# Row 28 of K and the last row copies in an adaLN block: from SBUF ahead of attention to DRAM and the first attention steps

## The chip, the cores and the metric

The kernel runs on one core of a Trainium2 chip. The metric is the device time of one launch in microseconds (us), as the median of several runs. The core has five engines that run their own instruction streams: PE (TensorE, matmuls), DVE (VectorE), ACT (ScalarE), POOL (GpSimd) and SP (SyncE). SP only issues DMA transfers here; sixteen DMA engines carry them. A stream runs in order, and an instruction waits for semaphores that other streams and transfers raise.

## What is computed

One transformer block with adaptive layer norm over 2048 tokens of width 448, in float32 (cut to what matters):

```
mod = (silu(c) @ w_mod).reshape(1, 6, 1, 448)       # sa, ca, ga, sb, cb, gb
h = layernorm(x) * (1 + ca) + sa
q, k, v = split(h @ wqkv)                           # 16 heads of width 28
p = softmax(q @ k.T * 28 ** -0.5)
x = x + ga * ((p @ v) @ wo)
h = layernorm(x) * (1 + cb) + sb
x = x + gb * (gelu(layernorm(h) @ w1 + b1) @ w2 + b2)
```

## The kernel before

Matmuls are done to nearly float32 accuracy with operands split in a high and a low part: three products instead of one.

**Phase 1** (to about 170 us) goes through the tokens in four blocks of 512 and computes Q, K and V. Heads are taken in four groups of four. In a group's tile of 128 rows, head j has rows 32j to 32j + 27. Q's four groups and K's groups 0 to 2 are projected directly; the four spare rows of each 32 in these seven carry pieces of K's fourth group, which is put together from them by copies inside DRAM. V stays in SBUF. High and low parts of Q and K go to DRAM arrays `dscr[kind][part][g]` (kind 0 is Q, 1 is K; part 0 is high, 1 low), which the order below calls d000 to d113, in that order of digits.

Three helpers of this phase issue on SP's queue:

- `put_spare` copies the spare rows of the groups and parts that were stored since the last call into the two arrays of K's group 3 (d103 and d113), one transfer of 4 x 4 x 512 for each part. `qk_task` calls it after it has stored a block, so each task's rows are copied one task later.
- `put_ones(g)` writes ones into row 28 of each head of group g in K's high part. They stand there because of the maxima: softmax subtracts a row's maximum, and that maximum, negated, is put in row 28 of Q (`max_fin`, L512), so that the score matmul itself subtracts it. The ones come from a strip of four partitions of the SBUF tile d0, read eight times over.
- `put_last_rows` does the same for group 3, in block 1 of phase 1.

The tile d0 is also scratch for some of phase 1's maxima, and in attention it is the first of three tiles (d0, c0, c1) that take the exponentials.

**Attention** has 16 units (four groups by four blocks of 512 queries) of 16 steps, each step 128 keys. In a step PE computes scores for two heads at a time (L1163, three products; the first has 29 rows, with the ones and the maxima), ACT takes the exponential into the tile (L1168, two to a step), and PE multiplies the step before's exponentials with V (L1133). There are two score tiles, s1 and s0, in turn, in the banks that phase 1's projections used. In between PE and DVE compute the maxima of groups to come, three or four in a step (`emit_max`: matmul L466, reduction L471). Step 0 also holds the last V projection task, on PE behind both score tiles.

Work is put at a step with a table: `at(step, fn)`, and `sched` is read at the end of each step's code. SP has no steps: its stream is the transfers in the order in which the code issues them. K is loaded by `load_k` (L653), Q of a unit by `load_q`, the high parts for the maxima by `load_hi` (L494), the output weights `wo` by a `Prep` object (four transfers for each of four groups, into three buffers `raw`).

**Lanes.** SP's transfers count on eight semaphores, DMAHW0 to DMAHW7, in turn: a transfer's lane is the one after its predecessor's. A transfer waits for the earlier one on its own lane, where that isn't known to be done, and for lanes of transfers whose data it reads or overwrites.

Between phase 1 and attention the code of before issues `load_hi` for what is deferred, then:

```
    put_spare()
    put_ones(1)
    put_ones(2)
```

The ones of group 0 are put in phase 1, in the third task of the last block.

Of the kernel before, what the change touches and what calls it, by code (L numbers as in the profile page):

```python
# [13 lines left out]
F32 = mybir.dt.float32  # L14
# [7 lines left out]
S = 2048  # L22
D = 448
H = 16
DH = 28
# [14 lines left out]
def tile_adaln_block(ctx: ExitStack, tc: tile.TileContext, x, wqkv, wo, w1, b1, w2, b2, c, w_mod, out):  # L40
    nc = tc.nc
    pe, act, dve, pool, sp = nc.tensor, nc.scalar, nc.vector, nc.gpsimd, nc.sync
# [22 lines left out]
    dr = ctx.enter_context(tc.tile_pool(name="dr", bufs=1, space=DRAM))  # L65
# [4 lines left out]
    def nm(t):  # L70
        uid[0] += 1
        return f"{t}_{uid[0]}"

    def sbt(tag, shape, dt=F32, bufs=1):
        return sb.tile(shape, dt, tag=tag, name=nm(tag), bufs=bufs)
# [32 lines left out]
    def f(t):  # L108
        return t.bitcast(F32)
# [226 lines left out]
    def v_init(i):  # L336
# [4 lines left out]
    dscr = [  # L341
        [[dr.tile([128, S], F32R, tag=f"d{kind}{part}{g}", name=f"d{kind}{part}{g}", bufs=1) for g in range(NG)] for part in range(2)]
        for kind in range(2)
    ]
# [5 lines left out]
    def by_head(t):  # L350
        return t.rearrange("(j r) n -> j r n", r=32)

    ones = d0[0:4, 0, 128:384]
    pool.memset(ones, 1.0)

    def put_ones(g):
        sp.dma_start(
            f(dscr[1][0][g])[DH:128:32, :].rearrange("j (q r) -> j q r", r=256),
            ones[:, None, :].broadcast_to([4, 8, 256]),
        )  # L360


    spare = []
# [1 line left out]
    def put_spare():  # L365
        for kind, g, sl in spare:
            n = 4 * (4 * kind + g)
            for part in range(2):
                sp.dma_start(
                    by_head(f(dscr[1][part][3]))[:, n : n + 4, sl], by_head(f(dscr[kind][part][g]))[:, DH:32, sl],  # L370
                )
        spare.clear()


    def put_last_rows():
        for part in range(2):
            sp.dma_start(
                by_head(f(dscr[1][part][3]))[:, DH:32, :].rearrange("j r (q n) -> j (r q) n", n=256),
                ones[:, None, :].broadcast_to([4, 32, 256]),
            )  # L380

    def mm_acc(p, terms, mid=None):
        for i, (a, b) in enumerate(terms):
            if mid and i == len(terms) // 2:
                mid()
            pe.matmul(p, a, b, start=(i == 0), stop=(i == len(terms) - 1))  # L386
# [11 lines left out]
    def qk_terms(b, kind, g, ps=None):  # L398
        ts = terms448(
            *hT[b],  # L400
            lambda k: wq[kind][0](k)[:, 128 * g : 128 * g + 128], lambda k: wq[kind][1](k)[:, 128 * g : 128 * g + 128],
        )
        return (ps or ps_s)(), [(w, h) for h, w in ts]

    def qk_task(b, kind, g, begun=None):
        p, ts = begun or qk_terms(b, kind, g)
        if begun is None:
            mm_acc(p, ts, p1_n[3])
        emit_task(*p1_n[:3])
        if g == 0:  # L410
            tg = ("kh" if kind else "qh") + str(b)
            hi = sb.tile([128, 512], F32R, tag=tg, name=nm(tg), bufs=1)
            (kh_sb if kind else qh_sb)[(g, b)] = hi
        elif g == 1 and b < 2:

            hi = sbt("raw" if kind else "osb", [128, 512], F32R, bufs=3 if kind else 2)
            (kh_sb if kind else qh_sb)[(g, b)] = hi
        else:
            hi = sbt("hi", [128, 512], F32R, bufs=3)
        full = sbt("full", [128, 512], bufs=3)  # L420
        lo = sbt("lo", [128, 512], F32R, bufs=3)
        act.copy(full, p)

        def split():
            (act.copy if b else dve.tensor_copy)(hi, full)
            if kind == 1 and (g, b) == (0, 1):
                k_diff.append(sbt("raw", [128, 512], F32R, bufs=3))
                pool.tensor_tensor(out=k_diff[0], in0=f(hi), in1=f(kh_sb[(0, 0)]), op=ALU.subtract)
            pool.tensor_tensor(out=lo, in0=full, in1=f(hi), op=ALU.subtract)
            sl = slice(b * 512, (b + 1) * 512)  # L430
            for part, t in enumerate((hi, lo)):
                sp.dma_start(f(dscr[kind][part][g])[:, sl], f(t))

            if (b, kind, g) != (3, 0, 3):
                put_spare()
            spare.append((kind, g, sl))

        return split
# [51 lines left out]
    def load_hi(kind, g, b):  # L490
        tg = ("kh" if kind else "qh") + str(b)
        t = sb.tile([128, 512], F32R, tag=tg, name=nm(tg), bufs=1)
        (kh_sb if kind else qh_sb)[(g, b)] = t
        sp.dma_start(f(t), f(dscr[kind][0][g])[:, b * 512 : (b + 1) * 512])  # L494
# [81 lines left out]
    def emit_task(n, sixth, n_pairs):  # L576
        if not n:
            return
        pairs = [pxq.pop(0) for _ in range(min(n_pairs, len(pxq)))]
        rests = [pair_diff(*m) for m in pairs]  # L580
        js = [m[3] for m in pairs]
        n_ops = n - len(pairs) + (sixth and len(pairs) > 0)
        singles = []
        for x in range(n_ops - len(pairs)):
            if mxq:

                free = [j for j in range(4) if j not in js] or range(4)
                fits = [y for y, m in enumerate(mxq[:16]) if m[:3] == mxq[0][:3] and m[4] == free[x % len(free)]]
                singles.append(mxq.pop(fits[0] if fits else 0))
        ops = [lambda ps, m=m: max_one(*m, ps) for m in singles]  # L590
        ops[2:2] = rests
        for x, op in enumerate(ops):
            op(ps_o if x + len(pairs) == 5 else ps_mx)
        for g, qt, cch, i, j in singles:
            count(g, qt, [cch])
        for g, qt, i, j in pairs:
            count(g, qt, [0, 1])
# [98 lines left out]
    for b in range(NB):  # L696
# [12 lines left out]
        for n, (tb, kind, g) in enumerate(tasks):  # L709
# [45 lines left out]
            if b == 1 and n == 8:  # L755
                put_last_rows()
# [10 lines left out]
            if not more:  # L767
                if n == 0:
                    load_q(0)
                    load_q(1)  # L770
                if n == 4:
                    load_k(0, 0)
                    load_k(0, 1)
                if n == 5:
                    act.activation(cols[:, 0:1], zero_col, AF.Exp)
                if n == 2:
                    put_ones(0)
# [29 lines left out]
    phase1[0] = False  # L807
    for item in deferred:
        load_hi(*item)
    put_spare()  # L810
    put_ones(1)
    put_ones(2)
    for g in range(1, NG):
        for qt in range(NB):
            for cch in range(NB):
# [245 lines left out]
    def at(step, fn):  # L1061
        sched.setdefault(step, []).append(fn)
# [10 lines left out]
    def b2_mul():  # L1073
        b2_row = sbt("row_b2g", [128, D])
        pool.tensor_tensor(out=b2_row, in0=rows["b2"][:, :D], in1=rows["gb"], op=ALU.mult)
        rows["b2g"] = b2_row

    at(12, b2_load)
    at(28, b2_mul)
    last0 = NKT * (NU - 1)  # L1080
# [41 lines left out]
    def n_maxima(s_):  # L1122
        n_plain, n_wo = left_steps(s_)
        over = len(mxq) - 7 * n_plain // 2
        if is_wo(s_):
            return max(0, -(-over // max(n_wo, 1)))
        plain[0] += 1
        return 4 if plain[0] % 2 or (over > 3 * n_wo and over > 0) else 3
# [11 lines left out]
    for u in range(NU):  # L1140
        g, qt = divmod(u, NB)
        for kt in range(NKT):
# [10 lines left out]
            n = n_maxima(step)  # L1153
# [81 lines left out]
    for n in range(len(seq) + LAG):  # L1235
        if n < len(seq):
            b, i = seq[n]
# [53 lines left out]
```

## Time and profile before

| | us |
|---|---|
| median of 3 runs | 1146.52 |
| lowest and highest run | 1146.39, 1147.67 |
| the profiled execution, its own time | 1146.45 |
| its span in the trace | 1144.7 |
| PE busy in the span | 1127.3 |
| DVE busy | 833.4 |
| ACT busy | 671.1 |

The profiled execution's time is 1.75 us above its span. Busy times are sums over the whole span, and PE's matmuls are pipelined, so that a busy PE is not PE at its peak. The page also gives the span in 40 equal slices of 28.6 us: the busy share of each engine in tenths, and the clock granted to PE. A wait is idle time of an engine right before an instruction, put down to what was last to end by the trace among the things that it waits for. SPq is SP's queue of DMA issues; a row of it is the issue, not the transfer.

### The profile page before, as it was taken

The page shows a single profiled execution, that of the slowest core. Times are in us where ns is not written, and L with a number is a line of the kernel's source. Part 1 is how long each engine was busy: PE and PEld are TensorE (multiplying, and loading weights), DVE is VectorE, ACT ScalarE, POOL GpSimd, SP SyncE. Part 2 cuts the span into 40 slices and gives each one's busy share as a digit, 9 for nine tenths or more (in the row PEclk, how much of TensorE's full clock was granted, in tenths as well). Part 3 has the DMA queues.
Part 4 walks back from the last instruction along what each step waited for, and adds up shares of the span by engine and source line. Part 5 has one row for each costly group of instructions (what it writes and reads, how often), then busy time and mean ns, then how long its engine had stood idle before and what let it go on. Part 6 is the DMA issues. An engine that isn't in the chain of part 4 may idle for free.

```text
span 1144.7 us, 20656 instructions
## 1 busy us (share of the span) xinstructions
PE 1127.3 (98%) x8319; PEld 674.3 (59%) x8319; DVE 833.4 (73%) x1485; ACT 671.1 (59%) x823; POOL 209.6 (18%) x211
## 2 busy tenths in 40 slices
PE   9999998999999999999999999999999999999998
PEld 6756663444444444444444444545458888888887
DVE  6869775999989989998989877586438853444322
ACT  5556655777878787887778777576862321211110
POOL 2533331210000000000000010207114503123000
PEclk9999998999999999999999999999999999999999
DMA  8562262111231211221111222020423100000000
GB/s 309 199 205 86 87 209 75 47 57 57 66 103 49 61 44 38 75 76 57 58 48 44 89 74 75 12 84 1 127 58 92 43 33 1 1 33 1 33 1 33
DMA packets 49389, 81.16 MB, mean 71 GB/s; under 512 B 12307, under 2 KB 18762, under 8 KB 49294
## 3 DMA queue, kind: packets, MB, share of 16 engines
q1 hardware_dynamic: 48810, 79.11, 21.9%
q8 instruction: 65, 1.06, 0.4%
q10 hardware_dynamic: 148, 0.46, 0.1%
q0 software_dynamic: 336, 0.28, 0.1%
q14 instruction: 30, 0.25, 0.1%
HBM read 54.94 MB, written 26.45 MB: 71 GB/s over the span
## 4 chain that ended last, share of the span: by engine, by line
PE 92%; DVE 3%; DMA 3%; ACT 1%; issue 1%; SPq 1%; POOL 0%; DVEq 0%; POOLq 0%; ACTq 0%
PE s L1163 27%; PE o L1133 21%; PE m L386 16%; PE pa L386 8%; PE m L466 6%; PE s L1226 4%; PE s L1227 4%; PE s L1225 4%; DVE mxp L471 2%; PE o L267 1%; DMA slot_c<-in_w_mod_dram 1%; PE ma L466 1%; DMA osb<-drec 1%; DMA drec<-den 0%; DMA d<-d 0%
## 5 line engine op out<-in xcount | busy, mean ns | idle before, releaser
L471 DVE TENSOR_REDUCE mxp<-m 128x1 f32<-128x512 f32 x884 | 558.4, 684 | 102.5 <-PE m L466 81.3
L1163 PE MATMUL s<-slot_b,slot_a 28*128 28x512 f32 (+1 forms) x3072 | 385.9, 424 | 7.0 <-ACT slot_d L1168 5.6
L1168 ACT ACTIVATE slot_c<-s 128x1024 f32<-128x1024 f32 x340 | 329.7, 1022 | 84.3 <-PE s L1163 84.2
L1163 PEld LDWEIGHTS s<-slot_b,slot_a 28*128 28x128 f32 (+1 forms) x3072 | 217.9, 185 | 258.6 <-ACT slot_c L1168 150.3
L466 PE MATMUL m<-kh,qh 28*128 28x512 f32 x863 | 287.7, 473 | 0.7 <-DVE mxp L471 0.4
L1168 ACT ACTIVATE slot_d<-s 128x1024 f32<-128x1024 f32 x172 | 166.7, 1021 | 51.4 <-PE s L1163 41.2
L1133 PE MATMUL o<-slot_c,v 128*32 128x512 f32 x1360 | 181.2, 605 | 0.0
L1209 ACT ACTIVATE full<-m,b_col 128x512 f32<-128x512 f32 x56 | 38.5, 688 | 191.9 <-PE m L386 179.7
L1212 DVE CAST hi<-full 128x512 fp32r<-128x512 f32 x56 | 25.2, 450 | 134.8 <-ACT full L1209 134.8
L466 PEld LDWEIGHTS m<-kh,qh 28*128 28x128 f32 x863 | 114.6, 182 | 8.8 <-DVE mxp L471 4.9
L899 POOL TENSOR_TENSOR osb<-osb,osb 128x512 f32<-128x512 f32 x16 | 20.9, 1308 | 448.9 <-DMA osb<-drec 327.8
L1133 PE MATMUL o<-slot_d,v 128*32 128x512 f32 x688 | 93.4, 610 | 0.4 <-ACT osb L1102 0.4
L386 PE MATMUL m<-y,slot_a 128*128 128x512 f32 x160 | 60.6, 395 | 0.0
L1133 PEld LDWEIGHTS o<-slot_c,v 128*32 128x32 f32 x1360 | 26.8, 108 | 53.9 <-issue 52.8
L1213 DVE TENSOR_TENSOR lo<-full,hi 128x512 fp32r<-128x512 f32 x56 | 44.2, 789 | 5.9 <-DVE hi L1212 0.9
L386 PE MATMUL m<-y,slot_c 128*128 128x512 f32 x152 | 47.5, 396 | 0.1
L1227 PE MATMUL s<-slot_v,lo 128*128 128x448 f32 x128 | 46.7, 365 | 0.0
L1225 PE MATMUL s<-slot_v,hi 128*128 128x448 f32 x128 | 46.6, 364 | 0.0
L471 DVE TENSOR_REDUCE mxp<-ma 128x1 f32<-128x512 f32 x54 | 35.6, 683 | 7.2 <-PE m L466 4.9
L386 PE MATMUL m<-y,slot_v 128*128 128x512 f32 x112 | 39.2, 396 | 0.0
L386 PE MATMUL m<-y,slot_b 128*128 128x512 f32 x112 | 39.0, 397 | 0.0
L479 ACT ACTIVATE slot_d<-m 128x512 f32<-128x512 f32 x33 | 18.7, 596 | 31.7 <-PE m L466 16.3
(249 smaller groups left out, 1410.0 us busy)
## 6 DMA issues: line engine op xcount, KB each, us to landing
slot_b<-d SPq DMA_DIRECT2D x32, 256.0 KB
slot_a<-d SPq DMA_DIRECT2D x32, 256.0 KB
d<-lo SPq DMA_DIRECT2D x28, 256.0 KB
d<-hi SPq DMA_DIRECT2D x16, 256.0 KB
osb<-drec SPq DMA_DIRECT2D x15, 256.0 KB
out_dram<-xn SPq DMA_DIRECT2D x16, 224.0 KB
raw<-in_B_w_dram SPq DMA_DIRECT2D x14, 224.0 KB
qh<-d SPq DMA_DIRECT2D x12, 256.0 KB
```

The source lines that it names most:

```text
L386: pe.matmul(p, a, b, start=(i == 0), stop=(i == len(terms) - 1))
L466: pe.matmul(m, qh_sb[(g, qt)][js, i * 128 : (i + 1) * 128], k[js, :], start=True, stop=True)
L471: dve.tensor_reduce(out=mxp[(g, qt)][:, i, j, cch : cch + 1], in_=m, op=ALU.max, axis=AX.X)
L1133: pe.matmul(o[32 * j : 32 * j + 32, :], v_sb[kt // 4][:, kt % 4, 4 * g + j, :], p[:, j, :], start=(kt == 0), stop=(kt == NKT - 1),)
L1163: pe.matmul(s2[:, jj, :], ks[rows_, kp, kc], qs[rows_, qp, :], start=(term == 0), stop=(term == 2))
L1168: act.activation(pt[:, 2 * hf : 2 * hf + 2, :], s2, AF.Exp, scale=SCALE)
L1209: act.activation(gf, p, AF.Gelu_apprx_tanh, bias=b1_col[:, i : i + 1])
L1212: dve.tensor_copy(ghi, gf)
L1213: dve.tensor_tensor(out=glo, in0=gf, in1=f(ghi), op=ALU.subtract)
L1225: pe.matmul(pp, ghi[:, ts], w_hi, start=(m == 0), stop=False)
L1226: pe.matmul(pp, ghi[:, ts], w_lo, start=False, stop=False)
L1227: pe.matmul(pp, glo[:, ts], w_hi, start=False, stop=(m == NFT - 1))
```

## The change

Three things are changed.

1. The ones get a copy in DRAM, `ones_d` (4 rows of 2048). It is filled by one more transfer from d0, right behind `put_last_rows` in block 1. `put_ones` copies from `ones_d`: 4 rows of 8 KB instead of 32 pieces of 1 KB out of d0.
2. In the last block `put_spare` is left out after K's task of group 2 too (after Q's task of group 3 it was left out before). What is left after phase 1 is then six copies instead of four; they are issued in attention step 1.
3. `put_ones(1)` and `put_ones(2)` move to attention steps 4 and 6.

```diff
@@ -353,11 +353,10 @@
     ones = d0[0:4, 0, 128:384]
     pool.memset(ones, 1.0)
 
+    ones_d = dr.tile([4, S], F32, tag="ones", name="ones_d", bufs=1)
+
     def put_ones(g):
-        sp.dma_start(
-            f(dscr[1][0][g])[DH:128:32, :].rearrange("j (q r) -> j q r", r=256),
-            ones[:, None, :].broadcast_to([4, 8, 256]),
-        )
+        sp.dma_start(f(dscr[1][0][g])[DH:128:32, :], ones_d)
 
 
     spare = []
@@ -378,6 +377,7 @@
                 by_head(f(dscr[1][part][3]))[:, DH:32, :].rearrange("j r (q n) -> j (r q) n", n=256),
                 ones[:, None, :].broadcast_to([4, 32, 256]),
             )
+        sp.dma_start(ones_d.rearrange("j (q n) -> j q n", n=256), ones[:, None, :].broadcast_to([4, 8, 256]))
 
     def mm_acc(p, terms, mid=None):
         for i, (a, b) in enumerate(terms):
@@ -431,7 +431,7 @@
             for part, t in enumerate((hi, lo)):
                 sp.dma_start(f(dscr[kind][part][g])[:, sl], f(t))
 
-            if (b, kind, g) != (3, 0, 3):
+            if b < 3 or g < 2 or (kind, g) == (0, 2):
                 put_spare()
             spare.append((kind, g, sl))
 
@@ -807,9 +807,6 @@
     phase1[0] = False
     for item in deferred:
         load_hi(*item)
-    put_spare()
-    put_ones(1)
-    put_ones(2)
     for g in range(1, NG):
         for qt in range(NB):
             for cch in range(NB):
@@ -1075,6 +1072,9 @@
         pool.tensor_tensor(out=b2_row, in0=rows["b2"][:, :D], in1=rows["gb"], op=ALU.mult)
         rows["b2g"] = b2_row
 
+    at(1, put_spare)
+    for g in (1, 2):
+        at(2 + 2 * g, lambda g=g: put_ones(g))
     at(12, b2_load)
     at(28, b2_mul)
     last0 = NKT * (NU - 1)
```

No instruction of PE, ACT, DVE or POOL is added, removed or moved; SP has one transfer more (458 for 457). Three places of the order follow, with what each row waits for.

ACT around the first exponential of attention (step 0), before:

```order
L448 COPY v3_228<-pa_480_2011 128x16x28 [waits PE_49]
L1168 ACTIVATE slot_d0_484_2048<-s1_485_2049 128x1024 [waits DMAHW5_49,DMAHW6_49,DMAHW1_49,DMAHW7_49,DVE_49,PE_49]
L1168 ACTIVATE slot_d0_484_2048<-s0_488_2063 128x1024 [waits PE_49,Activation_49]
L448 COPY v3_228<-m2_491_2077 128x16x28 [waits PE_49]
L1168 ACTIVATE slot_c0_497_2109<-s1_498_2110 128x1024 [waits PE_49]
```

and now:

```order
L448 COPY v3_228<-pa_480_2011 128x16x28 [waits PE_49]
L1168 ACTIVATE slot_d0_484_2042<-s1_485_2043 128x1024 [waits DMAHW0_49,DMAHW7_49,DVE_49,PE_49]
L1168 ACTIVATE slot_d0_484_2042<-s0_488_2057 128x1024 [waits PE_49,Activation_49]
L448 COPY v3_228<-m2_491_2071 128x16x28 [waits PE_49]
L1168 ACTIVATE slot_c0_497_2103<-s1_498_2104 128x1024 [waits PE_49]
```

The order is the same; the first exponential waits for two lanes instead of four. The transfers that now read d0 last stand in block 1 of phase 1: `L376 DMA d113_244<-slot_d0_4_86 4x32x256` and behind it `L380 DMA ones_d_246<-slot_d0_4_86 32x1x256 [waits DMAHW0_49]`, on lanes 7 and 0.

SP at the first K loads, at the end of phase 1 (slot_a2 is K's first 512 keys, slot_b0 the first unit's Q, full the negated maxima), before:

```order
L369 DMA d103_240<-d002_231 4x4x512 [waits DMAHW2_49,DMAHW0_49]
L369 DMA d113_244<-d012_235 4x4x512 [waits DMAHW3_49,DMAHW1_49]
L653 DMA slot_a2_461_1926<-d100_237 128x512 [waits PE_49]
L653 DMA slot_a2_461_1926<-d110_241 128x512
L653 DMA slot_a3_462_1929<-d100_237 128x512 [waits DMAHW4_49]
L653 DMA slot_a3_462_1929<-d110_241 128x512 [waits DMAHW5_49]
L512 DMA slot_b0_417_1752<-full_463_1932 4x4x32 [waits DMAHW6_49,DVE_49]
```

and now:

```order
L653 DMA slot_a2_461_1926<-d100_237 128x512 [waits DMAHW2_49,DMAHW1_49,PE_49]
L653 DMA slot_a2_461_1926<-d110_241 128x512
L653 DMA slot_a3_462_1929<-d100_237 128x512 [waits DMAHW3_49]
L653 DMA slot_a3_462_1929<-d110_241 128x512 [waits DMAHW4_49]
L512 DMA slot_b0_417_1754<-full_463_1932 4x4x32 [waits DMAHW5_49,DVE_49]
```

The two row copies ahead of the K loads are gone. Of the first K load's new waits, lane 2 is that of the ones copy for group 0, seven transfers earlier: `L359 DMA d100_237<-ones_d_246 4x2048 [waits DMAHW4_49]`.

SP behind the last deferred query load (qh0), where attention begins, before:

```order
L494 DMA qh0_481_2032<-d001_230 128x512 [waits DMAHW0_49,PE_49]
L369 DMA d103_240<-d102_239 4x4x512 [waits DMAHW1_49]
L369 DMA d113_244<-d112_243 4x4x512 [waits DMAHW2_49]
L369 DMA d103_240<-d003_232 4x4x512 [waits DMAHW3_49]
L369 DMA d113_244<-d013_236 4x4x512 [waits DMAHW4_49]
L357 DMA d101_238<-slot_d0_4_86 4x8x256 [waits DMAHW5_49]
L357 DMA d102_239<-slot_d0_4_86 4x8x256 [waits DMAHW6_49,DMAHW1_49]
L842 DMA raw_495_2097<-in_A_wo_dram 28x448 [waits DMAHW7_49,Pool_49]
```

and now (x4 is four transfers; without the waits):

```order
L839 DMA raw_496_2097<-in_A_wo_dram 28x448 x4
L368 DMA d103_240<-d002_231 4x4x512
L368 DMA d113_244<-d012_235 4x4x512
L368 DMA d103_240<-d102_239 4x4x512
L368 DMA d113_244<-d112_243 4x4x512
L368 DMA d103_240<-d003_232 4x4x512
L368 DMA d113_244<-d013_236 4x4x512
L839 DMA raw_524_2237<-in_A_wo_dram 28x448 x4
L359 DMA d101_238<-ones_d_246 4x2048
L839 DMA raw_539_2309<-in_A_wo_dram 28x448 x4
L359 DMA d102_239<-ones_d_246 4x2048
L494 DMA qh1_546_2339<-d001_230 128x512
```

Two groups of `wo` loads (eight transfers) stand between that query load and the row copies now; the ones copies stand behind the third and the fourth group.

## The prediction

> **What bounds the kernel now.** I read the page's head first.
>
> ```profile
> span 1144.7 us, 20656 instructions
> PE 1127.3 (98%) x8319; PEld 674.3 (59%) x8319; DVE 833.4 (73%) x1485; ACT 671.1 (59%) x823; POOL 209.6 (18%) x211
> PEclk9999998999999999999999999999999999999999
> ```
>
> PE is busy in 98% of the span, so time can only come from where PE stands still or runs slowly. The clock row has one 8, the seventh slice (171.7 to 200.3 us), where the projections end and attention begins. Then PE's own waits:
>
> ```profile
> PE s L1163 <- ACT slot_d L1168: 5.6, 1, 5.6
> PE pa L301 <- POOL cst L117: 1.4, 1, 1.4
> PE s L1163 <- DMA slot_b<-full: 1.2, 1, 1.2
> ```
>
> The first is one wait of 5.6 us, four times the next; the third lies just ahead of it. So I took the timeline of PE and ACT there (start, duration, instruction; in brackets the idle time before it and its releaser):
>
> ```profile
> 168.11 0.53 ACT L448 COPY v<-pa 128x448 f32<-128x448 f32 x1 [0.67 <-PE pa L386]
> 169.23 0.50 PE L1163 MATMUL s<-slot_b,slot_a 29*128 29x512 f32 x2 [1.16 <-DMA slot_b<-full]
> 173.58 0.72 PE L466 MATMUL m<-kh,qh 28*128 28x512 f32 x2
> 178.80 1.02 ACT L1168 ACTIVATE slot_d<-s 128x1024 f32<-128x1024 f32 x1 [10.16 <-DMA raw<-in_A_wo_dram]
> 179.87 0.79 PE L1163 MATMUL s<-slot_b,slot_a 29*128 29x512 f32 x2 [5.58 <-ACT slot_d L1168]
> ```
>
> Step 0's scores start at 169.23 us and PE has done all of step 0 by 174.30 (173.58 + 0.72). Step 1 needs the score tile back, which ACT frees by step 0's first exp; that starts only at 178.80. The exp writes the tile d0, where the ones lie, and the order in the section on the change shows its waits: lanes 5 and 6 are those of the ones copies for groups 1 and 2. The bracket names a wo load because that landed last by the profile. The chain of waits and SP's timeline show why those copies were late:
>
> ```profile
> 166.18 2.86 DMA slot_b<-full
> 170.92 4.62 DMA d<-d
> 175.55 0.26 SPq L357
> 175.91 2.90 DMA raw<-in_A_wo_dram
> ```
> ```profile
> 156.59 0.47 SPq L357 DMA_DIRECT2D d<-slot_d  x1
> 161.06 1.29 SPq L369 DMA_DIRECT2D d<-d  x2
> 162.41 1.88 SPq L653 DMA_DIRECT2D slot_a<-d  x4
> 164.39 2.31 SPq L512 DMA_DIRECT2D slot_b<-full  x4
> 170.50 0.38 SPq L494 DMA_DIRECT2D qh<-d  x1
> 170.92 3.33 SPq L369 DMA_DIRECT2D d<-d  x4
> 174.34 1.47 SPq L357 DMA_DIRECT2D d<-slot_d  x2
> 175.91 8.93 SPq L842 DMA_DIRECT2D raw<-in_A_wo_dram  x16
> 199.56 0.35 SPq L494 DMA_DIRECT2D qh<-d  x1
> ```
>
> Ahead of the ones stand the query load and four row copies, and the last ones copy waits for a row copy of the same group, in flight for 4.62 us. It goes out at 175.55; the exp starts 3.25 us later.
>
> The stall has a second price. Each row of the next view is a stretch of the program: the stall, steps 1, 2 and 3, and, for comparison, steps 5, 6 and 7 (busy times by engine, then PE's granted clock, DMA share and GB/s).
>
> ```profile
> 168.00:169.20 1.20, 0.07 (x1) 0.00 (x0) 0.00 (x0) 0.53 (x1) 0.00 (x0) 1.00 0.92 356
> 174.40:177.00 2.60, 0.00 (x0) 0.00 (x0) 1.00 (x2) 0.00 (x0) 0.00 (x0) 0.90 0.47 161
> 174.30:179.87 5.57, 0.00 (x0) 0.00 (x0) 1.10 (x2) 1.07 (x2) 0.00 (x0) 0.69 0.46 135
> 179.87:185.08 5.21, 5.08 (x23) 1.87 (x23) 1.98 (x3) 3.34 (x4) 3.10 (x4) 0.50 0.34 82
> 185.08:188.12 3.04, 3.04 (x29) 1.53 (x26) 2.17 (x4) 1.35 (x2) 0.00 (x0) 0.73 0.10 31
> 188.12:190.64 2.52, 2.52 (x27) 1.12 (x23) 2.27 (x4) 2.04 (x3) 0.00 (x0) 1.00 0.00 0
> 193.39:195.60 2.21, 2.21 (x29) 0.99 (x25) 1.95 (x4) 1.40 (x3) 0.00 (x0) 1.00 0.00 0
> 195.60:198.35 2.75, 2.75 (x30) 1.24 (x26) 2.43 (x5) 2.48 (x3) 0.00 (x0) 1.00 0.02 6
> 198.35:200.55 2.20, 2.20 (x28) 0.98 (x24) 2.17 (x6) 1.40 (x3) 1.45 (x3) 1.00 0.00 1
> ```
>
> While PE stands still its granted clock falls from 1.00 to 0.50. From 0.90 over 174.4 to 177.0 the fall comes at about 176.5 (2.1 us at 1.00 and 0.5 at 0.50 give 0.90), 2.2 us after the last matmul. Step 1 runs wholly at half clock, step 2 partly. Steps 1 to 3 take 5.21 + 3.04 + 2.52 = 10.77 us; steps 5 to 7, which hold the same 3, 4 and 3 maxima, take 7.16. The 1.2 us without matmuls before 169.23 left the clock at 1.00.
>
> **The change part by part.**
>
> *The stall.* The first exp no longer waits for late copies: its lanes are now 0 and 7, those of the last transfers that read d0, the second L376 copy and the L380 copy behind it. Before, that pair (L377) went out at 85.15 us:
>
> ```profile
> 85.15 0.86 SPq L377 DMA_DIRECT2D d<-slot_d  x2
> 99.38 0.34 SPq L432 DMA_DIRECT2D d<-qh  x1
> ```
>
> The exps can then run at about 170 and 171 us, under the last projection task, and step 1 follows step 0 at once: 5.6 us go. Next late would be ACT's copy of that task's values (0.5 us), which PE needs for a maximum in step 1; it now comes right behind the matmuls and was waited for before as well, so I price it at nothing.
>
> *The clock.* Without the stall PE's longest pause here is the 1.2 us one, which kept the clock. Steps 1 to 3 then cost what steps 5 to 7 do: 10.77 - 7.16 = 3.6 us go. [...]
>
> *VectorE.* The pause let it catch up; now it does not. It owes 1.10 us of reductions at the end of step 0 (row 174.30:179.87) and is busy 6.55 us in steps 5 to 7: together 7.65 in 7.16 us. Bounds: nothing, if it stays as far behind as it was, and 0.5 us lost. I take 0.25, the middle. Later it has room:
>
> ```profile
> 200.00:300.00 100.00, 100.00 (x952) 45.02 (x946) 91.54 (x156) 79.41 (x84) 12.44 (x16) 1.00 0.17 52
> 162.34 0.21 DVE L509 STREAM_TRANSPOSE full<-m 128x32 f32<-128x32 f32 x1
> ```
>
> With 8% idle it makes up any lag, so the gain is not given back by a bound VectorE.
>
> *The row copies moved from before the K loads.* The two at 161.06 (1.29 us) leave, so the K loads can issue at 161.06 instead of 162.41. The maxima's transfers (L512) behind them have their data early enough: the transpose ended at 162.55. But the K load reads the ones of group 0, now copied from DRAM. That copy is not in the trace; below it is the old ones copy's 3.25 us, above it the row copies' 4.62, DRAM to DRAM too. I take 4.62, the nearer kind: 156.59 + 4.62 = 161.2. From the first K load to the landing of the last maxima passed 6.63 us (162.41 to 166.18 + 2.86), so they land at 167.8. Then another thing is late, ACT's value copy, which frees the score tile's banks at 168.64. Scores start 0.19 us after a release: 168.83 for 169.23. Gain 0.4; bounds 0 and 0.4.
>
> *SP's queue from 170 us on.* Behind the query load come now 8 wo loads (8.93/16 = 0.56 each), 6 row copies (3.33/4 = 0.83 each), 4 wo loads, a ones copy (1.47/2 = 0.74), 4 wo loads, a ones copy: 9.0 + 5.0 + 1.5 = 15.5 us, from 170.9 to about 186.4 us. The queue's next instruction is the query load that went at 199.56, when its tile was free; with PE 9.4 us earlier that is 190.2. So 3.8 us of idle queue hide everything; without that cover query loads and, behind them, step 16's maxima would slip by what was over. The added copy into DRAM falls into SP's idle time from 86.0 to 99.38. Cost nothing. The ones of groups 1 and 2 and the group 3 rows are read much later, from the same queue.
>
> *Sum*, on the profiled execution's 1146.45 us (span 1144.7 and 1.75 around it): 5.6 + 3.6 + 0.4 - 0.25 = 9.35, so 1137.1. The median of the runs is 0.07 above that execution: **1137.2 us**, a gain of 0.8%. Its own range is 1136.6 to 1138.5: the terms' bounds, and 1 us for work in steps 1 to 3 that now meets ACT or DMA.
>
> **The rivals.**
>
> *Only the stall goes.* In step 1 PE also waited for ACT, and early exps and maxima may keep steps 1 to 3 slow at full clock. Against it: steps 5 to 7 hold the same work with VectorE at 91%. Gain 5.6 to 6.0: 1140.7 us.
>
> *The wait gets another owner.* The order names lanes, not instructions, and if the exp did depend on a wo load, as the bracket says, it would still wait. For it: the bracket. Against it: a wo load writes neither d0 nor the scores. Its price is small, since the wo loads now go at 170.9 and land 2.9 us later, at 173.8: step 1 at about 174.9, gain 5.0 + 3.6, 1137.9 us. Were some other release held to the old time, nothing would be gained: 1146.5.
>
> *Slower: the K loads wait for the ones from DRAM.* The first K load now waits for the ones copy issued shortly before (lane 2), and L512 and the first scores stand behind it on the same queue. The copy has 4 rows of 8 KB where 32 pieces of 1 KB went before, among busy DMA engines. Scores start 6.8 us after it lands. A pause of over about 2.2 us brings the half clock back, so only the 5.6 us are there to be lost: scores 5.6 us late, a landing at 168.0, 11.4 us after issue, is where it decides. At 15 us after issue: scores at 178.4, 9.2 late, 3.6 us lost, 1150.1 us. Against it: the longest landing in these rows is 4.62 us.
>
> **How the numbers follow.** The forecast has 0.70 (the wo variant within it); only the stall 0.15; no change of note 0.05; slower 0.05; 0.05 for a larger gain, such as step 1 quicker than steps 5 to 7. The range from 1135.9 to 1140.9 takes in the first two. A measurement of this kernel tells about 0.2% (2.3 us) from no change: faster 0.90, same 0.05, slower 0.05.
>
> **What would show it.** Right: PE's 5.6 us wait is gone; the first exp starts near 170 us, ahead of the last value copy; the seventh digit of PEclk is 9; step 1 starts near 173.9 us and steps 1 to 3 take 7.2 to 7.7 us; SP's L653 loads start near 161.1; wo loads from 171 us on. Wrong: a new wait of PE at its first scores of over 2 us, a clock of 0.50 there, or a lane wait of the first exp that ends after 172 us.

## The result, and the profile after

The changed kernel takes 1139.07 us (median of 4 runs, 1138.16 to 1139.53) against 1146.45 us (4 runs, 1146.18 to 1147.67) of the kernel before on the same chip. The ratio is 0.9933, with a 95% interval of 0.9915 to 0.9950: 7.4 us faster, where 9.35 had been forecast (1137.2 us). The time lies within the range on record. The profiled execution took 1139.53 us. Its head, and PE's longest waits:

```profile
span 1137.7 us, 20658 instructions
PE 1125.7 (99%) x8319; PEld 674.4 (59%) x8319; DVE 833.1 (73%) x1485; ACT 671.3 (59%) x823; POOL 209.7 (18%) x211
PEclk9999999999999999999999999999999999999999
```
```profile
PE s L1163 <- DMA slot_b<-full: 1.5, 1, 1.5
PE pa L301 <- POOL cst L117: 1.4, 1, 1.4
```

The wait of 5.6 us is gone and the seventh digit of the clock row is 9. What now leads the list is the wait that came third before, for the maxima at the first scores, and it has grown from 1.2 to 1.5 us. The timeline of PE and ACT at the start of attention:

```profile
167.72 1.18 PE L386 MATMUL pa<-slot_e,slot_c 128*128 128x448 f32 x5
170.41 0.50 PE L1163 MATMUL s<-slot_b,slot_a 29*128 29x512 f32 x2 [1.51 <-DMA slot_b<-full]
171.42 1.94 ACT L1168 ACTIVATE slot_d<-s 128x1024 f32<-128x1024 f32 x2 [1.95 <-PE s L1163]
172.33 4.06 PE L386 MATMUL m<-slot_e,slot_c 128*128 128x448 f32 x11
176.32 0.50 PE L1163 MATMUL s<-slot_b,slot_a 29*128 29x512 f32 x1
176.42 0.53 ACT L448 COPY v<-m 128x448 f32<-128x448 f32 x1 [3.06 <-PE m L386]
179.84 0.50 PE L1163 MATMUL s<-slot_b,slot_a 29*128 29x512 f32 x2
182.58 0.50 PE L1163 MATMUL s<-slot_b,slot_a 29*128 29x512 f32 x2
184.74 0.50 PE L1163 MATMUL s<-slot_b,slot_a 29*128 29x512 f32 x2
```

The two exps of step 0 start at 171.42, right behind their scores and 5 us ahead of the last value copy (176.42); step 1 follows step 0 without a gap, at 176.32. But two things are longer than forecast. The last V projection task (172.33) takes 4.06 us where the same eleven matmuls took 2.50 before. And steps 1 to 3, from 176.32 to 184.74, take 8.42 us where 7.16 plus 0.25 had been forecast. For comparison the same matmuls before, the last projection of phase 1 and the last V task:

```profile
165.57 2.50 PE L386 MATMUL pa<-slot_e,slot_c 128*128 128x448 f32 x11
171.15 2.50 PE L386 MATMUL m<-slot_e,slot_c 128*128 128x448 f32 x11
```

The table by stretches of the kernel after (busy times by engine, PE's granted clock, DMA share, GB/s) shows that the first of the two is the clock, and that the second is not:

```profile
168.90:170.40 1.50, 0.00 (x0) 0.02 (x1) 0.00 (x0) 0.53 (x1) 0.00 (x0) 1.00 0.82 280
172.30:173.00 0.70, 0.67 (x2) 0.63 (x3) 0.70 (x2) 0.70 (x2) 0.00 (x0) 0.64 0.87 202
173.00:174.00 1.00, 1.00 (x4) 0.88 (x4) 0.47 (x1) 0.36 (x1) 0.00 (x0) 0.50 0.89 307
175.00:176.00 1.00, 1.00 (x4) 0.92 (x3) 0.00 (x0) 0.00 (x0) 0.00 (x0) 0.54 0.99 333
176.00:177.00 1.00, 1.00 (x6) 0.49 (x5) 0.16 (x1) 0.53 (x1) 0.00 (x0) 1.00 0.49 121
176.32:184.74 8.42, 8.31 (x73) 3.53 (x72) 7.15 (x12) 5.51 (x7) 3.11 (x4) 1.00 0.28 79
```

From about 172.5 to 175.9 the clock is 0.50; in steps 1 to 3 it is 1.00 throughout, and VectorE is busy for 7.15 of the 8.42 us.

SP's queue went nearly as forecast (start, duration of the issues):

```profile
157.55 0.57 SPq L359 DMA_DIRECT2D d<-ones_d  x1
161.69 2.24 SPq L653 DMA_DIRECT2D slot_a<-d  x4
164.02 2.34 SPq L512 DMA_DIRECT2D slot_b<-full  x4
171.43 6.50 SPq L839 DMA_DIRECT2D raw<-in_A_wo_dram  x8
177.98 3.68 SPq L368 DMA_DIRECT2D d<-d  x6
185.89 0.56 SPq L359 DMA_DIRECT2D d<-ones_d  x1
193.68 0.35 SPq L494 DMA_DIRECT2D qh<-d  x1
```

Phase 1 ran 0.8 us later from its first microseconds on in this execution (by the chain of waits a load of w_mod took 7.37 us for 6.58 before), so 161.69 answers to the 161.06 forecast, give or take that shift. The last ones copy was out at 186.4 and the next query load went at 193.68: 7 us of idle queue hide what was moved there.

### The profile page after: what moved, and what is told of

Its sections match the earlier page's. It is cut to its first block, busy times and chain, and to the rows that moved or that the text cites. A ratio compares the mean times of both kernels' runs of the same rounds, so it can differ in the third digit from the quotient of the medians.

```text
span 1137.7 us, 20658 instructions
## 1 busy us (share of the span) xinstructions
PE 1125.7 (99%) x8319; PEld 674.4 (59%) x8319; DVE 833.1 (73%) x1485; ACT 671.3 (59%) x823; POOL 209.7 (18%) x211
## 4 chain that ended last, share of the span: by engine, by line
PE 93%; DVE 3%; DMA 2%; ACT 1%; issue 1%; SPq 0%; POOL 0%; DVEq 0%; POOLq 0%; ACTq 0%
PE s L1163 27%; PE o L1133 22%; PE m L386 16%; PE pa L386 8%; PE m L466 6%; PE s L1226 4%; PE s L1227 4%; PE s L1225 4%; DVE mxp L471 2%; DMA slot_c<-in_w_mod_dram 1%; PE o L267 1%; PE ma L466 1%; PE m L267 1%; DMA drec<-den 0%; DMA osb<-drec 0%
```

## The experiments

The theory after this first look had three parts. The first exp had waited for the ones copies, because they read d0; the stall's second price was the half clock behind it; and what was missing from the gain stood at the first scores (a pause, with half clock behind it) and in VectorE. The rivals were that another part of the change had brought the gain, that steps 1 to 3 had been slow before from crowding and not from the clock, and that the shortfall lay elsewhere in the span.

All kernels were timed in five rounds, in three groups, each on a chip of its own; the kernel before had medians of 1148.49, 1148.13 and 1148.21 us there, so ratios are compared. This table puts together, from the timelines of one profiled execution each, the pause of PE ahead of the first scores, the duration of the last V task, of steps 1 to 3, the time from the end of phase 1's last projection to the start of step 4, and the span from there to its end (us; forecast for the kernel after: 22.57 - 9.35 = 13.22 in the fourth column):

| kernel | pause | V task | steps 1 to 3 | to step 4 | rest |
|---|---|---|---|---|---|
| before | 1.16 | 2.50 | 10.77 | 22.57 | 954.1 |
| e1, before with 34 matmuls in the stall | 3.24 | 4.47 | 7.04 | 27.53 | 953.1 |
| e6, before with 18 | 2.32 | 3.30 | 8.09 | 20.55 | 953.9 |
| e2, before with ones from DRAM | 2.08 | 4.47 | 8.42 | 17.25 | 952.8 |
| after | 1.51 | 4.06 | 8.42 | 15.84 | 953.0 |
| e7, after again | 0.65 | 2.50 | 8.41 | 13.42 | 953.0 |
| e10, after once more | 1.09 | 2.54 | 8.42 | 13.89 | 954.5 |
| e5, after with the copies kept | 2.11 | 3.86 | 8.42 | 16.24 | 953.3 |
| e11, the same again | 1.16 | 3.92 | 8.55 | 15.48 | 952.8 |
| e3, after with 8 matmuls in the pause | filled | 2.50 | 8.42 | 14.68 | 953.0 |
| e4, after with K's second load behind the maxima | none | 2.50 | 8.42 | 12.70 | 954.4 |
| e8, the same again | none | 2.52 | 8.42 | 12.72 | 953.1 |
| e9, e8 without step 0's maxima | none | 2.53 | 7.63 | 11.95 | 953.2 |

The last column scatters by 1.7 us over kernels that are alike from step 4 on, and between executions of one kernel (after: 953.0, 953.0, 954.5). So the 1.1 us by which the profile of after is shorter than that of before behind step 4 (954.1 to 953.0) is no more than that scatter, and the change works in the stretch of the fourth column.

The row of before is one execution too, and its pause is the shortest of three: up to the stall e1 and e6 run the code of the kernel before, and there the pause lasted 3.24 and 2.32 us and the V task 4.47 and 3.30 us, for 1.16 and 2.50. The granted clock was 0.50 there (174.6 to 179.1 in e1, 174.5 to 176.0 in e6). So the kernel before can lose the clock at its first scores as well as the changed one.

**Which part brings the gain (e2).** To the kernel before only the copy of the ones in DRAM is added; `put_spare` and `put_ones(1)`, `put_ones(2)` stay where they were.

```diff
+    ones_d = dr.tile([4, S], F32, tag="ones", name="ones_d", bufs=1)
+
     def put_ones(g):
-        sp.dma_start(
-            f(dscr[1][0][g])[DH:128:32, :].rearrange("j (q r) -> j q r", r=256),
-            ones[:, None, :].broadcast_to([4, 8, 256]),
-        )
+        sp.dma_start(f(dscr[1][0][g])[DH:128:32, :], ones_d)
...
+        sp.dma_start(ones_d.rearrange("j (q n) -> j q n", n=256), ones[:, None, :].broadcast_to([4, 8, 256]))
```

> The kernel before with the ones kept in DRAM and copied from there, and nothing moved: four row copies and the ones of groups 1 and 2 stay right behind the query load, ahead of the wo loads. Theory (what counts is that the tile d0 is free): the first exp starts right behind the first scores, and the time is that of the changed kernel, 1138 to 1140 us. Rival (moving the copies out of SP's queue is a part of the gain, through the K loads or the wo loads): over 1 us slower than the changed kernel, 1140.5 us or more.

Measured: 1139.78 us (1138.98 to 1141.09), ratio 0.9927 [0.9915, 0.9938]. PE's and ACT's timeline:

```profile
171.23 0.80 PE L1163 MATMUL s<-slot_b,slot_a 29*128 29x512 f32 x2 [2.08 <-DMA slot_b<-full]
172.91 1.94 ACT L1168 ACTIVATE slot_d<-s 128x1024 f32<-128x1024 f32 x2 [3.19 <-PE s L1163]
173.56 4.47 PE L386 MATMUL m<-slot_e,slot_c 128*128 128x448 f32 x11
```

The two exps of step 0 wait for their scores alone, and the stall is gone although the ones copies and row copies go out where they did before. Freeing d0 is what takes the wait away; moving the copies is not needed for that, and its own worth is below what two ratios of 0.9927 and 0.9933 tell apart. Here too the first scores wait, 2.08 us, and the clock is at half from the first of them on (0.50 over 171.2 to 173.5; 0.80 us for two matmuls that take 0.50).

**What the half clock behind the stall costs (e1, e6).** The kernel before keeps its stall, but PE is given matmuls to do in it, whose result nobody reads: 34 in e1, 18 in e6.

```diff
             if kt == 0:
                 o = ps_o()
+                if step == 0:
+                    for _ in range(34):
+                        pe.matmul(o[:, :128], ident, ident, start=True, stop=True)
```

> The kernel before, with 34 matmuls of 128x128 on the identity put behind step 0's last maxima, into the output tile that the next instruction on it overwrites; by the warm-up's 1.45 us for 10 records at half clock they fill some 5 us of the 5.6 us stall, and the stall itself stays. Theory (the stall has two prices, 5.6 us of standing still and 3.6 us of half clock behind it): the clock stays at 1.00, steps 1 to 3 take 7.2 to 8 us instead of 10.77, and the time falls by 2.8 to 3.6 us, to about 1143. Rival (steps 1 to 3 are slow since ACT and the first loads are late, not for the clock): the clock stays up, but the time stays within 0.5 us of 1146.5.

> The kernel before with 18 filling matmuls on the identity behind step 0 instead of 34: in the first filled run 34 made 68 records and ran for 9.74 us, 4.2 us over the stall, so 18 run for some 5.2 us and end inside it. Theory (the half clock behind the stall is a price of its own): the stall stays, the clock is back at 1.00 when step 1 starts, steps 1 to 3 take 7.0 to 8.0 us as they did in the first filled run (7.04), and the time falls by 2.8 to 3.6 us against the kernel before of this call. Rival (the clock is not what the early steps wait for): within 0.7 us of before.

Measured, e1: 1147.67 us (1145.83 to 1151.73), ratio 0.9996 [0.9987, 1.0006]. PE's timeline, and steps 1 to 3 as one stretch:

```profile
180.15 9.74 PE L1181 MATMUL o<-ident 128*128 128x128 f32 x68
```
```profile
189.82:196.86 7.04, 7.04 (x72) 3.09 (x72) 5.96 (x10) 4.97 (x6) 0.00 (x0) 1.00 0.01 2
```

I had mis-sized the filling: each of the 34 appears as two matmuls in the trace (and the rate I went by, 1.45 us for 10 records, stands at a clock of 1.00 in the trace of before, not at half), and with 9.74 us it ran some 4 us over the stall, so the total says nothing. The stretch does: with the clock at 1.00 in them, steps 1 to 3 take 7.04 us for 10.77, with the same maxima. The clock had not been held: the V task ahead of the filling ran at half clock here (0.50 over 174.6 to 179.1), and the clock came back within the filling (0.79 on average over it). The difference, 3.7 us, is near the forecast's 3.6, but the filling also left ACT and VectorE 4 us more to catch up, so it is an upper bound for the clock alone.

Measured, e6: 1145.62 us (1143.58 to 1149.13, 11 runs), ratio 0.9981 [0.9971, 0.9991]: 2.2 us faster (1.0 to 3.3 by the interval; 2.8 to 3.6 had been expected), though the stall is still there. PE's and ACT's timeline:

```profile
178.42 4.29 PE L1181 MATMUL o<-ident 128*128 128x128 f32 x36
181.30 1.94 ACT L1168 ACTIVATE slot_d<-s 128x1024 f32<-128x1024 f32 x2 [10.57 <-DMA raw<-in_A_wo_dram]
183.13 0.54 ACT L448 COPY v<-m 128x448 f32<-128x448 f32 x1
183.72 0.49 PE L466 MATMUL m<-kh,qh 28*128 28x512 f32 x1 [0.36 <-ACT v L448]
```

The filling fits now. Steps 1 to 3 take 8.09 us: 2.7 less than before, 1.05 more than in e1. That rest stands in step 1, where a maximum waits for ACT's value copy, which comes behind the late exps (183.13 behind 181.30). So steps 1 to 3 were slow from the clock in the main, and not from crowding; its part by itself is a gain that can be measured, and the rows bound it by 2.7 and 3.7 us.

**The pause at the first scores (e7, e10, e3, e4, e8).** e7 and e10 are the changed kernel unchanged, in the second and third group.

> The changed kernel once more, for a comparison on one chip with the next two. Theory (its runs differ by whether the pause of PE at the first scores, 1.5 us in its profile, makes the clock fall): 7.4 to 9.5 us faster than the kernel before of this call, with a pause of 1.2 to 2.1 us in the profile; where the granted clock of a run is 1.000 its time is about 1 us lower than where it is 0.999 or less. Rival (the forecast's sum, without a second drop): 9.3 us or more faster in all runs.

> The changed kernel again, beside the next run. Theory: 7 to 9.5 us faster than the kernel before of this call; runs with a granted clock of 1.000 between 1137.5 and 1139.5, and now and then one with 0.992 to 0.998 and 2 to 6 us more.

Measured, e7: 1139.44 us (1137.68 to 1145.17), 0.9932 [0.9914, 0.9950]; e10: 1138.50 us (1136.76 to 1141.45), 0.9915 [0.9901, 0.9930]. PE's timeline of e7, then of e10:

```profile
170.12 0.50 PE L1163 MATMUL s<-slot_b,slot_a 29*128 29x512 f32 x2 [0.65 <-ACT v L448]
172.03 2.50 PE L386 MATMUL m<-slot_e,slot_c 128*128 128x448 f32 x11
```
```profile
170.52 0.50 PE L1163 MATMUL s<-slot_b,slot_a 29*128 29x512 f32 x2 [1.09 <-DMA d<-hi]
172.43 2.54 PE L386 MATMUL m<-slot_e,slot_c 128*128 128x448 f32 x11
```

In these two executions the pause is shorter and the V task takes 2.50 and 2.54 us, in e7 at a clock of 1.00; in e7 the owner is ACT's value copy, as forecast, and the stretch to step 4 is 13.42 us for 13.22 forecast. So the first profile's 4.06 us are no fixed cost of the change: they stood behind a pause of 1.51 us, and not behind 0.65 and 1.09. A pause of 1.2 to 2.1 us had been expected of e7; it was 0.65. In e10 the bracket names a store (d<-hi), and not the maxima; why the scores should wait for it is not shown.

e3 fills the pause with eight matmuls that nobody reads, between the last projection of phase 1 and the first scores; e4, and e8 again in the second group, takes its cause away instead: K's second chunk of 512 keys (512 KB in high and low part) is loaded behind the four transfers of the maxima (2 KB each), not ahead of them.

```diff
+    po = ps_o()
+    for _ in range(8):
+        pe.matmul(po[:, :128], ident, ident, start=True, stop=True)
     phase1[0] = False
```
```diff
                 if n == 4:
                     load_k(0, 0)
-                    load_k(0, 1)
...
             if not more and n == 5:
+                load_k(0, 1)
                 load_k(0, 2)
```

> The changed kernel, with 8 matmuls of 128x128 on the identity between the last projection of phase 1 and the first scores, where PE paused for 1.5 us in its profile; they take about 1.2 us and write a tile that nothing reads. Theory (the 2 us that are missing from the forecast are a second clock drop: 0.50 from 172.5 to 175.5 us behind that pause): the clock keeps 1.00, the last projection task takes 2.5 us instead of 4.06, and the time is 1136.9 to 1138.2, in all runs alike. Rival (the pause and the drop are not connected, or the late scores are what costs): the drop is there again in some runs and the time is 1138.2 to 1139.5 as now.

> The changed kernel, with the load of K's second 512 keys moved behind the transfers of the maxima: two K loads (512 KB) instead of four stand ahead of those on the queue. Theory (the maxima land at 170.3 us because they queue behind 1 MB of K and the stores of the last tasks in the DMA engines; an earlier issue alone does not help): they land 1 to 1.5 us sooner, PE's pause at the first scores falls from 1.5 to 0.3 to 0.6 us, the clock keeps 1.00, and the time is 1136.5 to 1137.8. Rival (the landing is set by something behind them or by the DRAM copy of the ones): the pause stays over 1.2 us and the time is that of the changed kernel.

> The changed kernel with K's second 512 keys loaded behind the maxima, once more beside the changed kernel itself. Theory: 1.0 to 2.0 us faster than that, no pause at the first scores in the profile, and the last projection task at 2.5 us. Rival (the difference seen before was one of chips): within 0.6 us of it.

Measured, e3: five runs, of which one took 2453.40 us, for a cause that is not known. The other four took 1137.52 to 1139.87 us, with a median of 1138.6 where 1136.9 to 1138.2 had been expected, and a ratio of 0.9915 [0.9902, 0.9928]. Measured, e4: 1137.94 us (1136.89 to 1138.58), 0.9905 [0.9891, 0.9920]; e8: 1137.83 us (1136.66 to 1138.23), 0.9909 [0.9896, 0.9922]. PE's timeline of e3, then of e4:

```profile
169.64 2.05 PE L809 MATMUL o<-ident 128*128 128x128 f32 x16
173.51 2.50 PE L386 MATMUL m<-slot_e,slot_c 128*128 128x448 f32 x11
```
```profile
167.73 1.99 PE L386 MATMUL pa<-slot_e,slot_c 128*128 128x448 f32 x9
169.65 0.49 PE L1163 MATMUL s<-slot_b,slot_a 29*128 29x512 f32 x2
171.57 2.50 PE L386 MATMUL m<-slot_e,slot_c 128*128 128x448 f32 x11
```

With the pause filled the V task takes 2.50 us, but the filling lasts longer than the pause (2.05 us for 1.51) and gives part of it back. With the load moved there is no pause at all: the scores follow the projection at once. The maxima had gone out at 164.02 in the kernel after, 0.1 us after SP was done with the K loads and as their last reduction ended, so neither their data nor SP's queue held them long. In e8 they went out at 164.80, later than in e7 (164.36), and in e9 at 164.24, and yet nothing waited for them: with K's second load in front of them the scores paused for 1.51, 0.65 and 1.09 us (after, e7, e10), with it behind them not at all (e4, e8, e9). Moving the load brings 1.6 us by the medians of e8 and e7; their intervals overlap, so this is a tendency, but the scatter is plain: over all groups 13 runs of e4, e8 and e9 lie between 1136.65 and 1138.58 us, 16 of the changed kernel between 1136.76 and 1145.17.

**The moved row copies (e5, e11).** In the changed kernel the two row copies are put back ahead of the K loads, in the second group and again in the third.

```diff
-            if b < 3 or g < 2 or (kind, g) == (0, 2):
+            if (b, kind, g) != (3, 0, 3):
                 put_spare()
```

> The changed kernel with the two row copies put back ahead of the first K loads (four copies are left for attention step 1). The forecast's term of 0.4 us for moving them would make this 0.4 us slower than the changed kernel. Theory now (the maxima land when the DMA engines have worked off what stands ahead of them, whenever they are issued): the K loads issue 1.3 us later, the maxima land within 0.5 us of the same time, and the total is within 0.5 us of the changed kernel's.

> The changed kernel with the two row copies ahead of the first K loads again, for a second sample. If moving them is worth more than the forecast's 0.4 us through PE's pause at the first scores (2.1 us in the first sample against 0.7 and 1.5), this is 1 to 2 us slower than the changed kernel in the same call and its profile shows a pause of 1.8 us or more; if the first sample's 1.6 us was scatter of the clock, the two are within 0.6 us and the pauses overlap.

Measured, e5: 1141.01 us (1138.33 to 1145.91), 0.9946 [0.9927, 0.9966]; e11: 1139.65 us (1138.79 to 1142.48), 0.9928 [0.9915, 0.9940]. PE's timeline of e11, and two stretches of it:

```profile
169.92 0.50 PE L1163 MATMUL s<-slot_b,slot_a 29*128 29x512 f32 x2 [1.16 <-DMA slot_b<-full]
171.83 3.92 PE L386 MATMUL m<-slot_e,slot_c 128*128 128x448 f32 x11
```
```profile
169.90:171.80 1.90, 1.71 (x16) 0.96 (x16) 1.31 (x3) 0.89 (x1) 0.00 (x0) 1.00 0.77 122
171.80:175.70 3.90, 3.87 (x13) 3.00 (x13) 1.17 (x2) 1.06 (x2) 0.00 (x0) 0.60 0.92 293
```

In both groups the kernel with the copies kept is slower than the changed one beside it, by 1.6 and 1.2 us, and both profiles show a slow V task (3.86 us, and 3.92 at a mean clock of 0.60). The intervals overlap both times, so this points to a gain from this part of the change and does not show it. That it comes through the pause is open too: 1.8 us or more had been expected of e11, and its 1.16 us are within what the changed kernel has by itself (0.65 to 1.51). In e5 the time was expected within 0.5 us of the changed kernel's, and was not.

**VectorE (e9).** To e8, step 0's maxima are left for later steps; nothing is left out of the computation.

```diff
             if step == 0:
                 v_task(NB - 1, 3, ps_mx())
-                emit_max(2)
```

> The changed kernel with K's second 512 keys behind the maxima (as in the two runs before this), and without the two maxima that step 0 computes behind the last projection task; they are done in later steps. In the changed kernel step 1 takes 3.5 us, with VectorE reducing five maxima without a gap (3.08 us), two of them step 0's. Theory (the forecast's term for VectorE was too small: its backlog sets the pace of step 1): steps 1 to 3 fall from 8.4 to 7.2 to 7.7 us, and the time is 0.2 to 1.0 us under that of the kernel with the loads moved alone (1137.8), since two maxima are still to be done later. Rival (ACT's value copy sets step 1's pace): steps 1 to 3 stay at 8.2 us or more.

Measured: 1136.94 us (1136.65 to 1138.02), 0.9903 [0.9890, 0.9915], the lowest of all kernels, though e10 beside it has 0.9915 with an interval that overlaps. Among the versions run, this one and e8 are those to keep: both medians lie below the changed kernel's of their group. VectorE's timeline at step 1 in e8, then in e9:

```profile
175.11 3.08 DVE L471 TENSOR_REDUCE mxp<-m 128x1 f32<-128x512 f32 x5 [1.84 <-PE s L1163]
178.68 2.48 DVE L471 TENSOR_REDUCE mxp<-m 128x1 f32<-128x512 f32 x4 [0.49 <-PE m L466]
```
```profile
174.63 2.48 DVE L471 TENSOR_REDUCE mxp<-m 128x1 f32<-128x512 f32 x4 [1.90 <-PE m L466]
177.37 2.48 DVE L471 TENSOR_REDUCE mxp<-m 128x1 f32<-128x512 f32 x4 [0.26 <-PE m L466]
```

In e8 step 1 begins with reductions that belong to step 0: their maxima stand behind the V task on PE, and now nothing lies between that task and step 1. Five reductions of 0.62 us then follow each other, and PE's next maximum has to wait for its bank (0.40 us, by its weight load in e8's trace); step 1 takes 3.53 us (174.58 to 178.11). In e9 it takes 2.75, and steps 1 to 3 take 7.63 us for 8.42. The half clock is not needed to explain 8.42 us: e7 and e8 have 8.41 and 8.42 us at a clock of 1.00, e4 and e10 8.42 behind V tasks of 2.50 and 2.54.

## Why the prediction came out as it did

**The stall (5.6 us): right.** The wait went, the first exp runs right behind its scores, and e2 shows that it hung on d0 alone. The rival that a wo load holds the exp is refuted: those loads went out from 171.43 on, and the exp started at 171.42.

**The half clock (3.6 us): right.** e6's gain of 2.2 us with the stall left in shows the mechanism; the size lies between the 2.7 us of e6's steps 1 to 3 and the 3.7 us of e1's, and no total by itself confirms it. The rival of "only the stall" (1140.7 us) falls with them.

**VectorE (0.25, at most 0.5): right place, too small.** What was priced was a lag carried through steps 1 to 3. What happened is that the reductions of step 0 crowd into step 1. Steps 1 to 3 take 8.42 us where 7.41 were forecast, but step 0 loses what is now done in step 1: in e7 it takes 4.35 us (170.12 to 174.47) where 10.64 - 5.58 = 5.06 were left. The net is 8.42 - 7.16 - 0.71 = 0.55.

**First scores 0.4 us earlier: wrong, and this is the step that failed.** Two sentences stood behind it: that the maxima land 6.63 us after the first K load, and that PE's longest pause here, of 1.2 us or less, keeps the clock. The first took a time from issue to landing as fixed. In the chain of waits of the kernel after it is the landing that moved:

```profile
165.85 4.47 DMA slot_b<-full
170.32 0.09 issue
```

4.47 us where 2.86 had been read: the K loads went out earlier, as forecast, but the 2 KB transfers went out behind 1 MB of K, and the DMA engines were busy for 0.82 of the pause. From first K load to landing passed 165.85 + 4.47 - 161.69 = 8.63 us. The 2.86 us had themselves been one sample. In e6, and then in e1, with the code of before up to there, the same transfer took:

```profile
168.45 3.84 DMA slot_b<-full
```
```profile
168.50 3.87 DMA slot_b<-full
```

So the same load in front of the maxima does not fix when they land; what else makes the executions differ stays open. In the profile of after, PE paused for 1.51 us and not 0.76, and that pause was followed by half clock, which cost 1.56 us in the V task. In the profiled execution these make up the difference: 0.75 + 1.56 + 0.30 (VectorE beyond its 0.25) = 2.6, and 15.84 - 13.22 = 2.6. In e7, where the pause was 0.65 us, this step came out as forecast, and the stretch came within 0.2 us of its 13.22; in e10 the pause was 1.09 us. The text on record had named "a clock of 0.50 there" as a sign against it; it had expected it only behind a wait of over 2 us, from the one fall that the trace of before shows, 2.2 us into the stall.

**The slower rival: refuted.** The ones copy of group 0 went out at 157.55 and the K loads at 161.69, 0.63 us after the 161.06 forecast with a phase 1 that was 0.8 us late. SP's waits there name no copy of the ones, so it did not hold them. **SP's queue, priced at nothing: right**; the six row copies took 0.61 us each for 0.83 forecast, the eight wo loads ahead of them 0.81 for 0.56, and the eight behind them 0.42, so that in sum the queue was through at 186.4, as forecast.

So the forecast of 9.35 us compares two executions in which the clock survives the pause at the first scores, the profiled one of before and one like e7. The measured gains, 7.4 us in the result and 8.7 and 9.7 us in the groups of e7 and e10, come from medians over executions of both kinds, and on both sides: the kernel before had 1146.45 us beside the result and 1148.13 and 1148.21 in those groups. That the clock makes all of these differences is not shown; the changed kernel's runs with a mean clock of 1.000 alone lie between 1136.76 and 1139.88 us. The result lies above the forecast's own bounds of 1136.6 to 1138.5 us. That it is within the whole range is partly luck: the upper end, 1140.9 us, was there for the rival in which only the stall goes, and not for a second loss of the clock.

## What to carry to other kernels

A wait for "a DMA" right at the seam of two phases can be the reuse of a scratch tile that a late, unimportant copy still reads: a copy of the constant elsewhere was worth nearly all of this change (a ratio of 0.9927 for 0.9933). Where the profile shows half clock behind a stall, price the stretch behind it too (here 10.77 us for 7.04 at a clock of 1.00), and fill or empty that stretch in an experiment to see its worth. Put a small transfer that is waited for ahead of large ones (here 2 KB ahead of 512 KB, and no pause for 0.65 to 1.51 us), and do not take its time from issue to landing over from a single execution (here 2.86, 3.84, 3.87 and 4.47 us); and ask of a stall that is removed which work it had let another engine catch up on.

## What the hardware did that was not expected

A pause of some 1.2 us may cost the clock or not. Before, 1.16 us ahead of the first scores left it at 1.00; in e11 a pause of the same 1.16 us was followed by the V task at a mean of 0.60 (3.92 us for 2.50), after 1.9 us of scores at 1.00. After 0.65 us (e7) it stayed at 1.00, and after 1.09 us (e10) the V task took 2.54 us. After 1.51 us (after) the clock fell 2.1 us behind the start of the scores, after 2.08 (e2) it was at 0.50 with the first matmul; but after 2.11 us (e5), 2.32 us (e6) and 3.24 us (e1) the first two scores still took 0.49, 0.51 and 0.49 us, and the slow matmuls came behind them (V tasks of 3.86, 3.30 and 4.47 us). Once down, the granted clock stayed at 0.50 for 3.41 us in the kernel after (172.50 to 175.91) and for 10.24 us in the one before (176.46 to 186.70). The means of stretches give some 3.4 us in e6, 6.8 us in e2 (171.2 to 178.0) and, with no row for 179.1 to 180.1, 9.3 to 10.3 us in e1. The 6.8 and the 10.24 us are near two and three times 3.41 us; what sets these lengths is not shown. By the profiles of these kernels, one each, every pause named here of 1.51 us or more was followed by half clock (in e5, where the clock was not read, by the V task of 3.86 us), and one of the two of 1.16 us was. What else decides whether the clock falls, they do not show.

The whole-span clock of single executions moves as well: of e7's six runs the one of 1137.68 us had a mean granted clock of 1.000, the one of 1145.17 us 0.992. Where in the span that run lost it stays open, since no profile of it was taken.
